# Fused attention and two gated MLPs on one core: the reciprocal root of two blocks' norms as a power on GpSimd

## The chip, the cores and the metric

The kernel runs on one core of one Trainium2 chip (trn2). A core has four engines that compute, each with a queue of its own that it works through in order: TensorE (PE in the rows; PEld is its loading of weights), VectorE (DVE), ScalarE (ACT) and GpSimd (POOL). SyncE (SP) issues the transfers (DMA). They wait for each other by semaphores. The metric is the device time of one launch in microseconds, the median of several runs.

## The reference

A windowed attention (4 batches, 8 heads, 576 positions of 64), a root-mean-square norm and a gated MLP with SiLU over its 2304 tokens of 512, and a second gated MLP without a norm. Cut to what matters:

```python
def _attn_ref(q, k, v):
    scores = (1.0 / np.sqrt(D)) * np.matmul(q, k.transpose(0, 1, 3, 2))
    rel = pos[:, None] - pos[None, :]
    scores = np.where((rel >= 0) & (rel < 64), scores, -1000000000.0)
    attn = np.exp(scores - np.max(scores, axis=-1, keepdims=True))
    attn = attn / (np.sum(attn, axis=-1, keepdims=True) + 1e-09)
    return np.matmul(attn, v)

def _moe_ref(x, w_gate, w_val, w_out, rms_g):
    rms = np.sqrt(np.mean(x * x, axis=-1, keepdims=True) + 1e-06)
    xn = x / rms * rms_g
    g = xn @ w_gate
    silu = g * (1.0 / (1.0 + np.exp(-g)))
    return silu * (xn @ w_val) @ w_out

def _moe2_ref(x, w_gate, w_val, w_out):
    gate = 1.0 / (1.0 + np.exp(-(x @ w_gate)))
    return gate * (x @ w_val) @ w_out
```

The weights are 512 x 1536 (gate and value) and 1536 x 512 (out). The change touches the factor 1 / rms of the norm.

## The kernel before

**Tiles and stages.** The 2304 tokens are six blocks of 384. Activations lie with the features on the 128 partitions (four groups of 128) and the tokens along the row. Attention makes 128 tokens at a time: scores on TensorE (L406), softmax on VectorE and ScalarE (L413 to L431), transposes (L439) and the product with v (L476), whose output ScalarE copies (L478) and squares (L481). Then comes the norm, then the first MLP, then the second. Blocks 0 and 1 take their first MLP by plain products, gate and value for one slice of 128 features of the 1536 at a time (L576, 12 products of 128x384 for either, since each number is split into a high and a low half of 16 bits); the later blocks, and the second MLP, take a scheme of fewer products over pairs of blocks (L625 to L627, L782, L893).

**Weights.** The weights arrive in chunks of 1024 columns and are readied on the way: VectorE takes the largest magnitude of each partition (L244), GpSimd reduces it over the partitions (an all-reduce, L247), VectorE turns that into a power of two (L248 to L255), and ScalarE and VectorE split the chunk into two halves (L271 to L273 and L337, L339). In block 0 and 1's time VectorE does this for one chunk after another.

**The norm of blocks 0 and 1** is `rms_first`, called for 256 tokens and for 128 tokens of each block, so four times: TensorE sums the squares into one column for each 128 tokens (L519), VectorE scales the sum and adds 1e-6 (L521, tile ra, 128x2 or 128x1), and `rsqrt` turns it into the reciprocal root (tile ry): an integer estimate and two corrections, ten VectorE operations on 128x2 or 128x1 numbers (L446 to L456, helpers rh and rt). VectorE multiplies the identity by it (L527), TensorE spreads that over the partitions (L528), VectorE scales the activations (L531), and `split_first` makes their two halves (L536 on ScalarE, L537 on VectorE), which L576 reads. Blocks 2 to 5 use `rms_scale`, whose root over 128x384 stays on VectorE in either kernel.

**Gate and value.** For a slice f the products fill one of two banks of PSUM. ScalarE takes the tanh (L588), VectorE frees the gate's bank (L589) and the value's (L599), and ScalarE and VectorE split the result (L609, L610). The next slice's gate needs the bank that L589 frees, its value the bank that L599 frees.

**Order.** The text of the program does not set the order. A table of numbers (ORDER, 5478 entries) does: `arrange` lists the operations as they were written, reads the table and ties every operation to the one ahead of it on its engine. The table was made by a planner outside the file. GpSimd's queue holds the all-reduces (L247, L279, L653), and three large ones for later norms (L509). The tile mhalf, 128x1 numbers of -0.5, is set at L1055 and read by nothing before.

Of the kernel before, what the change touches and what calls it, by code (L numbers as in the profile page):

```python
# [112 lines left out]
def fused_kernel(ctx, tc, q, k, v, w_gate, w_val, w_out, rms_g, w2_gate, w2_val, w2_out, const16, const32, out, plan, asked):  # L113
# [1101 lines left out]
    'FmuT*1^i5rOwj$U6ooSbFDb1z%KCj;>Oj@xCuOr|w6#x}g!<|kE^_!VDivlw`_f~MLTw4ViQck`W37c2#6=Lf$=ljUA&6}iNTbl@4@|RxE56HLXk^)kH'
    'skz$Drxtaex1GP(5y_flEjk&+h5nU}2#&>oSZ@d6QvjqVrr()ivuc^J+OFCbL12oT-~YvQnk?Q8lWj5G>U)!Re(6{_8q=>V?9Ta%fmGj%uI&qUHMoLwv'
    'Y}AMgeHxMyb%d6?Q0w&lI_aLTc=2hJRhF4G-<g;s3m~}T0l~KiWYPT+D*wf0<uj^l1=9B1s=ufc9J9&PxQAf%bWCff&db0Nxc9&VR2##foF(+m1ySt_2'
    'ucgv{vU;iNLEFkg2NH6PhKOQK~ZMihdv_aI+LXxiA8(8!{srcv0(zkC7cRhsetf;{k~QsUt6mBGo8!q?AI<p$|btPE_YAr0SqYM3YoA?z~**g9u6Uglp'
    'V^`5JAXA(_6EMT9C-H8B%DNd@u?psob)uoP^iMJi7-6&EOpPa&rH)<vG8R-M$Y+NMO_4r&VmDdnT`9Q9f@0vSlDP_?HTfdpE7^^5cROH{s<NEMVNa<Cw'
    'B?H@-=A6RHC%+z*oUptzsYCIjJnNq*TXClYfZ$~woa_e~t=@ZqU;sCW+(_u+F6p$hZpm^B394oQ~1><Sn3+I<Wx}#>lg3;MP@g4e7Z#%3_24uj1N{L(D'  # L1220
    'JF#`O9n?BDH}X$90mv|___fuvWzVwh%i^sUoySq<)iFu3UH^$)=Jw)($z$)t&xRzf;jM+AgRT!f46~11I6pCQjr}Y8y^;FcF70&tZPV>{N1a&lYR%zS_'
    'SLpN`IQm*89`MJU1v#1)lU@;3-`JHJ@?S|4qnIhRh#1qbJuRyJU$4A;uiVzS4k#p^;G-%XieI4;^E4p_335BKc1aE*ZRlYx26%ge?Gr;=aW*GSt$eT+s'
    'WImVdWQBZXH;@kovDUHo4!+qB-d^svpH1l`B=FACFI4^!uXU8|jGbv6qKl@~msH(4X_Gvm@Uwae%KAs3Q&XnDWu*G`xHMeVPgs4i=dO!~9;K9NS>W2Oh'
    'Ycng)=q3Wrv04*1(%9phV7)7QR~57k4Tm4&OI-b1hvmT80t3e=;e$+0B^!0xf46wIKq!}YB-E^~Q41fVLUNkYLxX&y3j0w35S4KEf8p-q?;9Q#L6VCz)'
# [142 lines left out]
```

## Time and profile before

| what | us |
|---|---|
| median of three runs | 873.52 (873.34 to 874.28) |
| span of the profiled execution | 872.6 |
| TensorE busy | 846.4 (97%) |
| VectorE busy | 736.5 (84%) |
| ScalarE busy | 555.1 (64%) |
| GpSimd busy | 31.3 (4%) |

The profile is one execution. Busy time is the time in which an engine ran an instruction. Starts and durations of small instructions overlap by some 0.08 us, since the next one starts while the last one drains, so what an instruction costs its engine is read from its start to the next one's start. A row of the chain is a piece of the work that ended last, followed back from the end. "POOLq" is what GpSimd's sequencer does on its own, without its cores computing.

### The profile page before, as it was taken

How to read it: one execution, taken by the hardware profiler on the slowest of the kernel's cores; microseconds unless marked ns; L12 is line 12 of the kernel's file. 1: busy time of each engine (PE TensorE's matmuls, PEld its weight loads, DVE VectorE, ACT ScalarE, POOL GpSimd, SP SyncE). 2: the span in 40 equal slices, each digit the busy share in tenths (PEclk: the TensorE clock that was granted, in tenths of full speed). 3: DMA queues.
4: the chain of work that ended last, by engine and by line, in shares of the span. 5: the costliest groups of instructions: out<-in, count | busy, mean ns of one | idle time of the engine just before them, and what ended most of it. 6: DMA issues, size and time to landing. Idle time of an engine off the chain costs nothing.

```text
span 872.6 us, 15623 instructions
## 1 busy us (share of the span) xinstructions
PE 846.4 (97%) x6084; PEld 523.7 (60%) x6084; DVE 736.5 (84%) x1427; ACT 555.1 (64%) x1214; POOL 31.3 (4%) x42
## 2 busy tenths in 40 slices
PE   4599999999999999999999999999999999999998
PEld 3466666666666666656666666666566666666664
DVE  5999999899887897688889999989889787546695
ACT  5888877767577866356466576767667457335640
POOL 0000010101000101100000000000000000000000
PEclk9989999999999999999999999999999999999999
DMA  9666531232112033301423656527241112023034
GB/s 342 240 210 239 192 127 45 66 104 80 66 38 66 27 133 137 125 37 37 133 85 118 223 190 233 208 73 238 85 147 45 62 41 91 2 72 138 28 109 145
DMA packets 33193, 104.19 MB, mean 119 GB/s; under 512 B 3808, under 2 KB 11360, under 8 KB 27872
## 3 DMA queue, kind: packets, MB, share of 16 engines
q1 hardware_dynamic: 33120, 103.20, 34.0%
...
HBM read 82.35 MB, written 20.84 MB: 118 GB/s over the span
## 4 chain that ended last, share of the span: by engine, by line
PE 88%; DVE 8%; DMA 2%; ACT 1%; issue 0%; POOL 0%; SPq 0%; DVEq 0%; ACTq 0%; POOLq 0%
PE bank L782 45%; PE bank L893 14%; PE bank L576 10%; PE bank L625 4%; PE bank L626 4%; PE bank L627 4%; PE bank L406 2%; PE bank L476 2%; PE bank L439 1%; DMA att<-f 1%; DVE wmax L244 1%; DMA att<-in_q_dram 1%; DMA wl<-in_moe_w_gate_dram 1%; DVE wl L339 1%; DVE wl L273 1%
## 5 line engine op out<-in xcount | busy, mean ns | idle before, releaser
L782 PEld LDWEIGHTS <-wl 128*128 128x128 f16 x2520 | 246.0, 98 | 164.9 <-issue 2.1
L782 PE MATMUL bank<-att,wl 128*128 128x384 f16 x2016 | 338.1, 326 | 0.6 <-DVE att L710 0.3
L795 ACT ACTIVATE bank<-bank 128x384 f32<-128x384 f32 x120 | 56.9, 478 | 75.4 <-PE bank L782 31.3
L893 PEld LDWEIGHTS <-wl 128*128 128x128 f16 x756 | 74.0, 98 | 48.9
L576 PE MATMUL bank<-xhl,wl 128*128 128x384 f16 x576 | 97.6, 326 | 0.4 <-DVE th L589 0.4
L782 PE MATMUL bank<-xhl,wl 128*128 128x384 f16 x504 | 86.2, 326 | 0.6 <-DVE xo L785 0.6
L576 PEld LDWEIGHTS <-wl 128*128 128x128 f16 x576 | 55.5, 98 | 36.9 <-issue 1.3
L625 PE MATMUL bank<-wl,wl 128*128 128x384 f16 x192 | 62.7, 326 | 0.0
L626 PE MATMUL bank<-wl,wl 128*128 128x384 f16 x192 | 62.6, 326 | 0.0
L627 PE MATMUL bank<-wl,wl 128*128 128x384 f16 x192 | 62.6, 326 | 0.0
L337 ACT ACTIVATE wl<-wl,isc 128x1024 f16<-128x1024 f32 (+1 forms) x48 | 54.2, 1142 | 9.6 <-DVE wl L317 6.3
L893 PE MATMUL bank<-xhl,wl 128*128 128x384 f16 x264 | 51.6, 326 | 0.0
L244 DVE TENSOR_REDUCE wmax<-wl 128x1 f32<-128x1024 f32 x36 | 43.6, 1213 | 4.8 <-DMA wl<-in_moe_w_out_dram 2.5
L893 PE MATMUL bank<-wl 128*128 128x384 f16 x222 | 45.9, 326 | 0.0
L271 ACT ACTIVATE wl<-wl 128x1024 f32<-128x1024 f32 x36 | 41.4, 1153 | 6.5 <-DMA wl<-in_moe_w_out_dram 3.5
L429 ACT ACTIVATE sm<-sm,su 128x128 f32<-128x128 f32 x120 | 38.0, 388 | 8.9 <-DVE su L424 8.7
L422 ACT ACTIVATE sm<-sm,nm 128x128 f32<-128x128 f32 x96 | 37.3, 391 | 9.2 <-DVE nm L416 9.2
L627 PEld LDWEIGHTS <-wl 128*128 128x128 f16 x288 | 28.2, 98 | 18.6
L625 PEld LDWEIGHTS <-wl 128*128 128x128 f16 x288 | 28.2, 98 | 18.6 <-issue 1.2
L339 DVE SCALAR_TENSOR_TENSOR wl<-wl,isc,wl 128x1024 f16<-128x1024 f32 (+1 forms) x32 | 38.1, 1196 | 1.1 <-ACT wl L337 0.9
L626 PEld LDWEIGHTS <-wl 128*128 128x128 f16 x288 | 28.2, 98 | 17.2
L273 DVE SCALAR_TENSOR_TENSOR wl<-wl,wl 128x1024 int32<-128x1024 int32 x28 | 34.3, 1225 | 0.3
...
## 6 DMA issues: line engine op xcount, KB each, us to landing
wl<-in_moe_w_out_dram SPq DMA_DIRECT2D x15, 1024.0 KB, 5.4
wl<-in_moe_w_val_dram SPq DMA_DIRECT2D x13, 1024.0 KB, 5.2
wl<-in_moe_w_gate_dram SPq DMA_DIRECT2D x13, 1024.0 KB, 5.7
...
vn<-in_v_dram SPq DMA_DIRECT2D x27, 256.0 KB, 3.4
...
```

Source lines behind the costliest of these rows:

```text
L244: V.tensor_reduce(out=r1[:, i:i + 1], in_=wraw(layer, j + i)[:, :, 1].bitcast(F32), axis=AX.X, op=ALU.max, apply_absolute_value=True)
L271: A.activation(out=y.bitcast(F32), in_=hi.bitcast(F32), func=AF.Prelu, scale=2.0 ** -112, alpha=-2.0 ** 32)
L273: V.scalar_tensor_tensor(out=y if (layer, j) in PACKED else hi, in0=y, scalar=3, in1=lo, op0=ALU.logical_shift_left, op1=ALU.bitwise_or)
L337: A.activation(out=hi, in_=y, func=AF.Copy, scale=sc)
L339: V.scalar_tensor_tensor(out=lo, in0=y, scalar=sc, in1=hi, op0=ALU.mult, op1=ALU.subtract)
L576: T.matmul(pb[:, 0:n], lhsT=w_, rhs=x_, start=(c == 0), stop=(c == m - 1))
L625: T.matmul(o[c][:, 0:n], lhsT=wh[:, cs], rhs=hi, start=st, stop=False)
L626: T.matmul(o[c][:, 0:n], lhsT=wh[:, cs], rhs=lo, start=False, stop=False)
L627: T.matmul(o[c][:, 0:n], lhsT=wl[:, cs], rhs=hi, start=False, stop=en)
L782: T.matmul(pb[:, 0:NMAX], lhsT=w_, rhs=x[:, t, kk], start=first and kk == n == 0, stop=kk == 1 and n == 2, skip_group_check=not first)
L795: A.activation(out=o[:, 0:NMAX], in_=i[:, 0:NMAX], func=AF.Copy)
L893: T.matmul(pb[:, 0:NMAX], lhsT=w_, rhs=x[:, t], start=st and s == ss[0] and n == 0, stop=s == ss[-1] and n == 2, skip_group_check=not st)
```

## The change

In `rms_first` the call of `rsqrt` becomes one GpSimd instruction, a power: ra to the exponent -0.5, which is mhalf spread over the columns. It is L522 in either file, and is called four times. The ten operations L446 to L456 go from these four calls, and helpers rh and rt with them. The whole table ORDER is another one (its lines say nothing to a reader and are left out; of 5478 entries it places 4535 differently, by 12 places in the median).

```diff
--- before.py
+++ after.py
@@ -519,7 +519,7 @@
                 T.matmul(pb[:, i:i + 1], lhsT=sq_tile(blk, t0 + i)[:, c], rhs=ones[:, 0:1], start=(c == 0), stop=(c == KC - 1))
         a, y = small("ra", 3)[:, 0:nt], small("ry", 3)[:, 0:nt]
         V.tensor_scalar(out=a, in0=pb[:, 0:nt], scalar1=1.0 / DM, scalar2=1e-6, op0=ALU.mult, op1=ALU.add)
-        rsqrt(y, a, small("rh", 3)[:, 0:nt], small("rt", 3)[:, 0:nt], V)
+        G.tensor_tensor(out=y, in0=a, in1=mhalf.to_broadcast([P, nt]), op=ALU.pow)
 
         pb = abank(st, "r")
         for i in range(nt):
```

Since the buffers are numbered as they are made, names such as wmax_389 and wmax_367 are the same tile in both.

**GpSimd's queue from its first all-reduce.** Before, up to the third all-reduce (amax are the largest magnitudes of two weight chunks, gamr that of the norm's gain):

```order
L1302 MEMSET const-uint8-127 128x1
L1361 UNCONDITIONAL_BRANCH
L247 ISA
L247 ISA amax_83<-wmax_0_389 128x2
L279 ISA gamr_0_119<-gam_0_117 128x1
L247 ISA amax_83<-wmax_1_492 128x2
```

Now, from the third all-reduce to the seventh:

```order
L247 ISA amax_83<-wmax_1_470 128x2
L522 ISA
L522 TENSOR_TENSOR ry_1_356<-ra_1_355,mhalf_82 128x1
L522 TENSOR_TENSOR ry_0_305<-ra_0_304,mhalf_82 128x2
L247 ISA
L247 ISA amax_83<-wmax_0_367 128x2
...
L522 ISA
L522 TENSOR_TENSOR ry_0_305<-ra_0_304,mhalf_82 128x2
L247 ISA
L247 ISA amax_83<-wmax_1_470 128x2
```

An ISA row with no tile stands wherever a power follows an all-reduce or an all-reduce a power; there are six such rows besides the first one, and the kernel before has that first one alone. The power of block 1's first two tiles (ra_0_304) stands ahead of an all-reduce of two chunks that has no wait of its own, since it follows in the queue.

**VectorE's queue at block 0's norm.** Before, from the L521 of its first 256 tokens (ra_304, ry_305; ra_366, ry_367 are those of the third 128):

```order
L521 TENSOR_SCALAR ra_304<-bank_200 128x2
L272 TENSOR_SCALAR wl_76<-wl_76 128x1024
L446 TENSOR_SCALAR ry_305<-ra_304 128x2
L339 SCALAR_TENSOR_TENSOR wl_75<-wl_76,isc,wl_75 128x1024
L447 TENSOR_SCALAR ry_305<-ry_305 128x2
L521 TENSOR_SCALAR ra_366<-bank_126 128x1
L449 TENSOR_TENSOR rh_307<-ry_305 128x2
L446 TENSOR_SCALAR ry_367<-ra_366 128x1
```

Now, from the L521 of the third 128 tokens (now ra_355, ry_356):

```order
L521 TENSOR_SCALAR ra_355<-bank_126 128x1
L339 SCALAR_TENSOR_TENSOR wl_75<-wl_76,isc,wl_75 128x1024
L418 TENSOR_SCALAR nm_183<-nm_183 128x8
L527 TENSOR_SCALAR xhl_266<-ident,ry_356 128x128
L521 TENSOR_SCALAR ra_304<-bank_200 128x2
L339 SCALAR_TENSOR_TENSOR wl_75<-wl_76,isc,wl_75 128x1024
L527 TENSOR_SCALAR xhl_266<-ident,ry_305 128x128
```

The third tile comes first, and one L339 stands between each L521 and the L527 that needs its power.

**VectorE's queue at block 1's first norm call.** Before, from its L521 (th are gate and value results, wl2 weights and halves):

```order
L521 TENSOR_SCALAR ra_0_304<-bank_0_125 128x2
L589 SCALAR_TENSOR_TENSOR th_0_474<-th_0_474,bank_4_200 128x384
...
L446 TENSOR_SCALAR ry_0_305<-ra_0_304 128x2
L610 TENSOR_TENSOR wl2_76<-th_1_540,wl2_76 128x384
L447 TENSOR_SCALAR ry_0_305<-ry_0_305 128x2
...
L244 TENSOR_REDUCE wmax_0_389<-wl2_76 128x1
...
L273 SCALAR_TENSOR_TENSOR wl2_76<-wl1_75,wl2_76 128x1024
```

Now:

```order
L521 TENSOR_SCALAR ra_0_304<-bank_0_125 128x2
L244 TENSOR_REDUCE wmax_0_367<-wl2_76 128x1
L610 TENSOR_TENSOR wl2_76<-th_0_452,wl2_76 128x384
L272 TENSOR_SCALAR wl2_76<-wl2_76 128x1024
L248 TENSOR_SCALAR amax_83<-amax_83 128x2
L255 TENSOR_SCALAR tg1_86<-pw_84,pgam_81 128x1
L599 SCALAR_TENSOR_TENSOR th_1_518<-th_1_518,bank_5_206 128x384
```

The L248 now stands three rows behind the L244 that follows L521, and on GpSimd its all-reduce stands behind this call's power. L599 of the same slice follows it.

**VectorE's queue at block 1's second norm call.** Before, from the L244 of the chunk, with the L521 and the L527 of the call:

```order
L244 TENSOR_REDUCE wmax_1_492<-wl2_76 128x1
L339 SCALAR_TENSOR_TENSOR wl1_75<-wl2_76,isc_85,wl1_75 128x1024
...
L521 TENSOR_SCALAR ra_1_366<-bank_2_163 128x1
...
L599 SCALAR_TENSOR_TENSOR th_2_616<-th_2_616,bank_5_206 128x384
...
L456 SCALAR_TENSOR_TENSOR ry_1_367<-rh_1_369,ry_1_367 128x1
L527 TENSOR_SCALAR xhl_3_526<-ident_77,ry_0_305 128x128 x2
L589 SCALAR_TENSOR_TENSOR th_1_540<-th_1_540,bank_4_200 128x384
L527 TENSOR_SCALAR xhl_3_526<-ident_77,ry_1_367 128x128
```

Now, from the L244 to the L527:

```order
L244 TENSOR_REDUCE wmax_1_470<-wl2_76 128x1
L339 SCALAR_TENSOR_TENSOR wl1_75<-wl2_76,isc_85,wl1_75 128x1024
L589 SCALAR_TENSOR_TENSOR th_0_452<-th_0_452,bank_4_200 128x384
L610 TENSOR_TENSOR wl2_76<-th_1_518,wl2_76 128x384
L527 TENSOR_SCALAR xhl_3_504<-ident_77,ry_0_305 128x128
L248 TENSOR_SCALAR amax_83<-amax_83 128x1
L521 TENSOR_SCALAR ra_1_355<-bank_2_163 128x1
L599 SCALAR_TENSOR_TENSOR th_0_452<-th_0_452,bank_5_206 128x384
L423 TENSOR_SCALAR su_0_146<-su_0_146 128x8
L527 TENSOR_SCALAR xhl_3_504<-ident_77,ry_1_356 128x128
```

The L244's all-reduce, the power of ra_1_355 and the L527 that reads it (ry_1_356) are nine rows apart on VectorE, and the power stands on GpSimd behind that all-reduce and one ISA row.

## Rows read from the trace of the kernel before

**Rows 1.** The page's busy shares (1) and its chain by engine (4).

```profile
PE 846.4 (97%) x6084; PEld 523.7 (60%) x6084; DVE 736.5 (84%) x1427; ACT 555.1 (64%) x1214; POOL 31.3 (4%) x42
...
PE 88%; DVE 8%; DMA 2%; ACT 1%; issue 0%; POOL 0%; SPq 0%; DVEq 0%; ACTq 0%; POOLq 0%
```

**Rows 2.** Table by stretches: busy us of each engine, granted clock, DMA share, GB/s.

```profile
core 0: us, PE busy (x) PEld busy (x) DVE busy (x) ACT busy (x) POOL busy (x), PEclk, DMA share, GB/s
...
20.00:30.00 10.00, 5.42 (x48) 4.32 (x47) 10.00 (x25) 8.96 (x24) 0.73 (x1) 1.00 0.81 296
...
40.00:51.20 11.20, 7.54 (x80) 5.55 (x79) 11.12 (x36) 9.24 (x23) 0.72 (x1) 0.56 0.62 221
...
75.00:100.00 25.00, 25.00 (x216) 16.82 (x214) 24.87 (x58) 20.52 (x47) 1.09 (x3) 1.00 0.40 141
100.00:125.00 25.00, 25.00 (x210) 16.01 (x208) 24.68 (x59) 18.80 (x48) 2.15 (x3) 1.00 0.61 224
...
850.00:872.60 22.60, 19.07 (x118) 11.25 (x115) 13.00 (x24) 2.21 (x5) 0.00 (x0) 1.00 0.41 140
```

**Rows 3.** Chain of waits in the head: start us, us, what.

```profile
43.28 0.28 DVE xhl L527
...
51.30 8.72 PE bank L576 x53
```

**Rows 4.** The page's costliest groups (5): out<-in, count, busy us, mean ns, idle before.

```profile
L337 ACT ACTIVATE wl<-wl,isc 128x1024 f16<-128x1024 f32 (+1 forms) x48 | 54.2, 1142 | 9.6 <-DVE wl L317 6.3
...
L271 ACT ACTIVATE wl<-wl 128x1024 f32<-128x1024 f32 x36 | 41.4, 1153 | 6.5 <-DMA wl<-in_moe_w_out_dram 3.5
...
L339 DVE SCALAR_TENSOR_TENSOR wl<-wl,isc,wl 128x1024 f16<-128x1024 f32 (+1 forms) x32 | 38.1, 1196 | 1.1 <-ACT wl L337 0.9
```

**Rows 5.** VectorE's timeline, three places: start us, us, line, operation, out<-in.

```profile
85.28 0.55 DVE L610 TENSOR_TENSOR wl<-th,wl 128x384 f16<-128x384 f32 x1
85.75 0.15 DVE L449 TENSOR_TENSOR rh<-ry 128x2 f32<-128x2 f32 x1
85.82 1.22 DVE L244 TENSOR_REDUCE wmax<-wl 128x1 f32<-128x1024 f32 x1
86.95 0.16 DVE L450 TENSOR_TENSOR rh<-rh,ra 128x2 f32<-128x2 f32 x1
...
99.09 0.69 DVE L272 TENSOR_SCALAR wl<-wl 128x1024 int32<-128x1024 int32 x1
99.70 0.15 DVE L451 TENSOR_SCALAR rt<-rh 128x1 f32<-128x1 f32 x1
...
118.43 0.55 DVE L589 SCALAR_TENSOR_TENSOR th<-th,bank 128x384 f32<-128x384 f32 x1
```

**Rows 6.** TensorE's timeline, gate and value products from 111 us.

```profile
111.40 17.72 PE L576 MATMUL bank<-xhl,wl 128*128 128x384 f16 x108
```

**Rows 7.** The line of the all-reduces, L247: min/median/max ns, starts, who waited.

```profile
L247 POOL PARTITION_ALL_REDUCE amax<-wmax x30: 350/584/1311, 16.5 to 705.7; - x30
L247 POOLq MODIFY_POOL_CONFIG  x2: 11/11/11, 0.8 to 0.8; - x2
...
  DVE amax L248: 1.7, 5
```

**Rows 8.** GpSimd's timeline: start us, us, line, operation.

```profile
0.27 0.10 POOL L1302 MEMSET const-float32-1.0<- 128x1 f32 x1
...
16.48 0.81 POOL L247 PARTITION_ALL_REDUCE amax<-wmax  x1 [16.06 <-DVE su L423]
...
87.13 0.37 POOL L247 PARTITION_ALL_REDUCE amax<-wmax  x1 [10.29 <-DVE rh L450]
```

**Rows 9.** DMA issues of the first 60 us: KB each, median us to landing.

```profile
wl<-in_moe_w_gate_dram SPq DMA_DIRECT2D x5, 1024.0 KB, 5.7
...
att<-in_q_dram SPq DMA_DIRECT2D x6, 256.0 KB, 5.6
...
wl<-const SPq DMA_DIRECT2D x1, 128.0 KB, 2.0
```

More of the change, by code (lines that the diff above doesn't have):

```diff
@@ L1215 @@
[L1215 to L1224, printed above, removed]
@@ L1255 @@
[L1255 to L1259 removed]
+    'c-n1O2S5}@7rvR@+v6G>2X_Z3N0TBQLhl9?0Z~j8H5ywq8oMSY8jYzYL4Qj$CeheyEV0DirHBP3(g{)oL5lQ#Wq1As<Zk!y;P$r6o0;#u?|tvBSF>3&kjfBL'
@@ new lines @@
+    'LrbXPNuX1y1ANh7)c`+5Fdsrp%EcToE6ky`i88mYX^zH>F{%6>9Q8D8^c`uw7yn5Yj7p$xPC2vaFg5~{U?!LgCV^1cE9=2*A_0Yl!}BoV-fO$pSi+qcjTl$='
+    'h&3Z_QqJAbT~%xK?vqVRjI%@V8h)_@^eqm_Z49|(Vubr$_M;a!qM|Y>YiJ@e!W+z0V#Umq4x`<R+s%-o0$0AW>E)9`s+TVYo$_93lVIZY(GN{Zkx<lOYz*2>'
+    'JOIfB;vP}o4=$Di2%vF~Rzh(j;Qb(&7YNBKSln<F1E}3_-u|WN&v}np=t0q`eHP=did)RKrP$Sa#GD52p96S&I-&>^r%4qDJn?}lAw5|K-eE~`DV_&a+u$oC'
+    'yLtZ4v_PS}KmA0=GkPLiL}5_cg8N{vdTlWXC;@_B>;yO|>V6IVin{}2_bLR%4uuj0x7e@SI7h+d@o<Vqw#s0;qKS+1yKo>t2vb%oP1{X7wWcK3p&YmCN40aF'
@@ new lines @@
+    '07ISyz_V~9)d#X=7=|hVoSso-Q;qCG5!G{U)*I}$mE}&#+aL-{rJ@1O2h~b&YSs2+U`=L@ut-g62c{jjC!F)m8CRV<;h1pZ3xuIh_AI~<elg+KPxwivF~CJg'
+    'gTHqJK};Qc50AXx%|*v&f^OsBEWDYoIX)A|H4yShT#ex*4gr7=sf8*WLT7a;?znh2ns#dX@gFx#5x1I9YN4&D0Jkt}k#zb#6>>qRPlacj8U3Iuv>?1KUD7ED'
+    'ZIpIMTcsczTv5*g*Fr$jJv8w!NV*F;6UoeRfe*UHW6nrGrzE;X(kyF+Lf`yWJib#S<-RTmfA@maBTeci$!d;oHN~2w!B?k&6XVeJ(OI!JRqc|t&_}LRwSAQv'
+    'qPi&QaO3B#A|(_-Z95_F?T|vX{DnF4s-TJDo*`>>t+J7%Ms%vVLbb@g%!#V>?39quH`Tqs1Srk&T0eYd)}k^qLd~9yn7L<8Gpw~T8<y_{UbNvMg)Uf=9JQh7'
@@ new lines @@
+    'G>Os_Hba1k;qaQ4uukzq*T}ovm##JiVrW|+QktSd3oZ~iDjJ{_nMtFXohof}Y_C&DDg!FTidPD5Jy5Dz8@ohZB1z5g_XK-^QH?p6yU820fBl_t&@Gf0q<WnF'
+    'PWH;Q?1j4*KHa+3XUZAXb5Ld}EU)`?n?-|S!>RvV(i9CgRmrF2Yd_tU&v)vrEOJwFwbv#{9e2b(tFxSRHR-d66&32-<TKNAdG`My@1ji}iyJG0E?D|rDf;rf'
+    'C+|*plrZCQ&?6JeNU5s1KIvd|?-P47t`-n2V|FhDH)1;~)GzBlJmnSo$CG`HW%3*TPr89XZj%Q1F~;Wu+xA!dx^+|Xfw|P-#));r!*O+9MUUcpA14>u2`a5*'
+    'b<ZO*t^S_gDrk)Xe@z2t-v_PPe#5+TRB5ZT6cE8YTdrdxcu=~e)Rj)6CK2GKdP#w#+yT^C{=TsZn3cDS&0trT0%QgJ71!Dw-~vcc0s!y?xea1LFaOKQ5%rL7'
@@ new lines @@
+    '90&hNgm!V^0Hdbyj?A?EZ)EXtezH~X<liDd`acvlVM+9RVYFGom9;;EHBoW&>6P)+b0^9M2!LZ-`~N<-zC6hjV1(GVtlgwThN*{DFGSbk_mNI`@DV$HP)0a-'
+    'MmXco-KKv-+cr}ju3+ZRxJQA<hv>7dN6Y{ieJh^I56C9D`(Ceq2}UYse7}BEvxQ2_GaUx=++lKC0e<N-lT5z&f}>^K(`n$+M8Z1DN)0Z8DQz;ptoGPqM=qXD'
+    'XiPvrrwK-^4M#CjdZk*UwD4gkr_K#YNINu}zQzE#5`Peo6+uxMnGta$Fv3)T+cz@h8}NRS0GuSQKgkBV4~9_0{V)g!Eew4u>h>(-+XY-9!T2Lq^G`I16*s|H'
+    'lAq_6?ih&OI}N^lgrp8dQ4PYh1r_TLT}Zmu7}93iC?~yA7HR#m`RQ`klEl^FE_cV>AgQt8->=QE8(!{~0Yd~&18&G(3e7#H&xa-<$D<Y}xXE6%p1t$fxBlY%'
@@ new lines @@
+    'ihtD?e>}mT=zJVU^T>9SVh^Iu`{TObzuN^yj?8FEn32Bs#F1Z!NAUV9P*`Uv%bak>$VSldN^Sj5tXpPiq5RWrX!&|Y=R+h*{&LO{a`J<*Xn(&ao+L_$+9T#o'
+    'A0CA>4-w&)79EN$8TG4+>&@XGoTh3%mF^+!sWG=71&!G^`^OC>=~$ra<?&a+gK3jiSvZA*jTRL<*Z!P5J8#^Lglo!4o7QR}zRc=W4i>jj4SlT}&}{xWlfPz='
+    'yaO95Q4v`8o_qGS33JCk*zCJA^*_qeK1&f;R6ZkyIQ>$2Aqk$?l689g2mku23o3epN=KcMN4~;U+~@5f@}}6!50h*UtOQuoi$L3Q-i4(lHxiGf6k?C7&7=G`'
+    'Rc$N^{$lg(AL1gzw7D&#ww5`D_^*~lE|?y>V)Oi&5yUm(^DHfK=Rzu><)uX5io#A~)b?2?KG-Ytd?aW!RT-&PWrENxYi{OWY&E+Ws`&eU(TZ(uKi*1%8!3LS'
@@ L1260 @@
+    'tY&~+J6S$py|5S*T1Ipzpj&0&lv!a05A6o8ME&)R@fwBoiB|uo6R`<m&{J{xE47|}j5iLJ5*juz%;tfks}TeL1KdDpU@%*l3~Pa51I7UcjrM?A4AcpvD;kC`'
+    'LjMO`Dvy%'
 )
```

63 lines of the change are left out of this document (24 added, 39 removed).

## The prediction

> **What bounds the kernel now.** I read the page's busy shares and its chain first. TensorE is busy for 846.4 of 872.6 us and carries 88% of the chain that ended last, VectorE 8% [rows 1]. The table by stretches then says where TensorE's missing 26 us lie [rows 2]: in the head, up to its first gate product L576 at 51.30 us [rows 3], and in the last 22.6 us, where 3.5 us are missing. Between them TensorE is full. It is full there only because VectorE keeps up: VectorE is busy 11.12 of 11.2 us before the first L576, 24.87 of 25 us from 75 to 100 and 24.68 of 25 from 100 to 125 [rows 2]. The margin is read from two timelines. The 108 products from 111.40 us take 17.72 us, so the 12 of one bank 1.97, and the fifth dozen starts at 111.40 + 4 x 1.97 = 119.28 [rows 6]; the L589 that frees its bank ends at 118.43 + 0.55 = 118.98 [rows 5]. So TensorE is 0.3 us from waiting for VectorE. Up to about 127 us a microsecond of VectorE is a microsecond of the program; after that TensorE is full to the end, and what was lost or won stays.
>
> The profiled span is 872.6 us, the median of the runs 873.52. All sums below are differences, added to the median.
>
> **Part 1: forty VectorE instructions go.** Four calls of ten. One of them holds VectorE from 85.75 to 85.82, so 0.07 us from start to start, and now and then somewhat more for a turn of tiles [rows 5]: 40 x 0.075 = 3.0 us, half in the head, half between 82 and 102 us. At the tight places near 119 to 127 us the new order also keeps one L272 (0.61 us, from 99.09 to 99.70 [rows 5]) behind instead of ahead. VectorE thus has 3.0 to 3.6 us less to do before it frees those banks.
>
> **Part 2: the new order in the head.** Up to block 0's last L537 VectorE now has, besides the 20 instructions gone (1.5 us), two L244 (85.82 to 86.95, 1.13 us each), two L272, one L273 and one L339 (1.2 us [rows 4], the L273 alike) less in front: 1.5 + 2.3 + 1.2 + 1.2 + 1.2 and 0.2 of small ones = 7.6 us. ScalarE, which makes the squares that L519 sums and was busy 8.96 of 10 us in the stretch from 20 us [rows 2], sheds two L337 and one L271 there, 1.14 + 1.14 + 1.15 = 3.4 us [rows 4]. So VectorE will wait for ScalarE and TensorE in the head: not at all if ScalarE sets nothing, 7.6 - 3.4 = 4.2 us if it sets everything. Its products serve one of several steps there, so I take a third, 1.4 us. The first L576 should come 4 to 6 us earlier, near 46 us. This gain is mostly not kept: the work pushed behind the norm is still VectorE's, TensorE starts early and then meets the same evictions, which are only 3.0 to 3.6 us less late. Kept: 3.5 - 1.4 = **-2.1 us**. The order's shuffling after 130 us moves no work between engines; TensorE is full there, and I put it at nothing, within 2 us either way. The tail is the same chain of products, eviction and store.
>
> **Part 3: what the power costs on GpSimd.** The power itself is 128 x 1 or 128 x 2 numbers. No row shows it. The nearest are GpSimd's MEMSET of 128 x 1, 0.10 us [rows 8], and its all-reduces of 128 x 1 or 2, 0.35 to 1.31 us [rows 7]; I take 0.6 with the two hand-overs. That replaces a chain of ten instructions, and in the head an L339 (1.2 us) stands between each L521 and its L527, so it costs nothing there.
>
> The larger cost is not in the diff. In the changed order GpSimd has six more of the ISA rows that carry no tile, one wherever a power follows an all-reduce or the reverse; the kernel before has one, ahead of its first all-reduce. There the trace calls it MODIFY_POOL_CONFIG, 11 ns on GpSimd's sequencer at 0.8 us [rows 7]: GpSimd is switched to another set of routines. What such a switch costs until the next routine can run, call it X, lies between 0.011 us and the 15.65 us that pass from there to the first all-reduce at 16.48 us, which waited for its data, not for the switch [rows 7, 8]. If routines have to be fetched, the nearest rows are loads: 2.0 us for a small constant tile, 5.6 and 5.7 us for tiles of the first 60 us [rows 9]. I take X = 5.6, as most loads there take that, and as routines for a whole engine are not a small tile.
>
> The Trainium skill, GPSIMD Engine Reference, section 2.1 (Instruction dispatch), says that the first call to freshly loaded code pays some 6 us (5.95 measured) for loading, with no instruction to be seen. No row here shows it; with 5.95 in place of X the forecast below would be 880.1 us.
>
> Which switches are covered? In the head the switch before the first power has some 8 us between the all-reduce ahead of it and the L521 that it waits for, and the one after the second power some 7 us until the next L248 asks for an all-reduce: hidden at 5.6. In block 1 two are not.
> (a) L521 of the first two tiles, then a power, a switch, and the all-reduce of weight chunk 10, on which an L248 waits three VectorE instructions later: L244 1.13, L610 0.47, L272 0.61 [rows 5], 2.21 us of cover. Needed: 0.6 + X + 0.37 (an all-reduce like that at 87.13 [rows 8]). Exposed: X - 1.24.
> (b) The all-reduce of chunk 13 behind its L244, a switch, the power of the third tile, and its L527. In VectorE's queue between that L244 and that L527 stand an L339 (1.2 [rows 4]), three of 0.47 (L589, L610, L599) and four small ones, 3.0 us in all. Needed: 0.37 + X + 0.6. Exposed: X - 2.0.
> Behind both waiting instructions, in the same queue, stand L589 and L599, which free the banks of TensorE's gate and value products; nothing else covers them. Today all L248 together wait 1.7 us [rows 7]. Together 2X - 3.2, which is 8.0 us at 5.6. TensorE has more slack than 0.3 us at about 90 us, but by 119 to 127 us it has used it, so the wait arrives there whole.
>
> **Sum.** 873.5 - 2.1 + 8.0 = **879.4 us**. Every 1 us of X is 2 us; the sum is no change at X = 2.7.
>
> **Rivals.**
> *A, faster: the switch is short or fetched ahead.* If X is below 1.2 us both waits vanish in their cover and the 40 instructions are simply gone: 873.5 - 2.1 = 871.4, 870 to 872 by the head's term. For it: the one row there is reads 11 ns, and no queue of loads on the page is named for it. It decides from X below 1.7.
> *B, slower by more: the routines are fetched only when first called, not at the switch.* Then the cover ahead of a call is lost. In the head the first power of block 0 pays X + 0.6 less the L339 and L418 between its L521 and L527, 1.3: X - 0.7. In block 1 place (a) pays twice, 2X - 1.2, and at (b) only 0.6 us stand between L521 and L527: X. Together 4X - 1.9 = 20.5 us at 5.6, less 2.1: about 892, or 888 where TensorE's slack at 90 us takes some. For it speaks nothing in the trace: the first all-reduce took 0.81 us [rows 8], no longer than others, but it came long after the switch. The rule of that page of the skill, read by its letter (the first call pays), is this case.
> *C, no change: X near 2.7*, like the small constant's load [rows 9]: 871.8 to 875.3.
> *D, the gain is not there:* if the path in the head is ScalarE's and TensorE's wholly, 4.2 us are waited for instead of 1.4 and the kept gain is nothing: every case is 2 us later, A is C.
>
> **How the numbers follow.** Forecast, X from 3.5 to 8: 0.48. A 0.26, C and A with D 0.12, B 0.14. A measurement of this kernel can tell about 0.2%, 1.75 us, from no change, so faster (under 871.8) 0.26, same 0.12, slower 0.62. The forecast's own range is 875.5 to 885. For 8 in 10 the range has to take in most of A, so it starts at 870.5; B is left out above, and it ends at 885.5.
>
> **What would show it.** First L576 near 46 us (part 2). GpSimd idle between an all-reduce and the power, though the L521 has ended, by X; VectorE idle near 85 to 90 us ahead of an L248 by about 4.4 us, and near 103 to 107 us ahead of an L527 by about 3.6. TensorE idle before L576 between 90 and 127 us by some 6 us, and full after. If VectorE stands idle ahead of the first L527 of block 0, it is B. If VectorE waits nowhere for GpSimd, it is A. What would make all of it wrong: a fall of the granted clock after the new pauses (it stood at 0.56 over the sparse 40 to 51 us [rows 2]), or stages after 130 us whose new order makes TensorE wait.

## The result, and the profile after

The changed kernel takes 885.94 us (median of 4 runs, 884.86 to 886.3) where the kernel before takes 873.9 beside it: 1.0135 of its time, with an interval of 1.0121 to 1.0149, so 12.0 us slower. The direction was forecast and so was the mechanism; the size was not: 879.4 us was predicted, and the range ended at 885.5.

The page of the changed kernel, its busy shares and the group of the gate and value products:

```profile
PE 850.4 (96%) x6084; PEld 524.4 (59%) x6084; DVE 729.1 (82%) x1387; ACT 550.0 (62%) x1214; POOL 32.3 (4%) x46
...
L576 PE MATMUL bank<-xhl,wl 128*128 128x384 f16 x576 | 102.5, 336 | 4.0 <-DVE th L599 3.0
```

The span grew by 11.5 us, from 872.6 to 884.1. TensorE has the same 6084 products. It stands still for 884.1 - 850.4 = 33.7 us where it stood still for 26.2 [rows 1], so 7.5 us more, and it is busy 4.0 us longer with the same work.

The table by stretches of the changed kernel, with the columns of [rows 2]:

```profile
40.00:51.20 11.20, 11.20 (x108) 7.48 (x101) 10.81 (x19) 9.42 (x19) 0.62 (x1) 0.78 0.45 166
51.20:75.00 23.80, 22.62 (x192) 14.12 (x190) 23.80 (x42) 20.61 (x45) 0.71 (x2) 1.00 0.58 214
75.00:100.00 25.00, 21.83 (x184) 14.33 (x183) 19.80 (x36) 18.43 (x51) 1.79 (x3) 0.93 0.47 162
100.00:125.00 25.00, 16.35 (x138) 10.30 (x137) 14.08 (x33) 9.47 (x25) 1.61 (x3) 0.80 0.38 127
```

Three things stand in it. VectorE, which was busy 24.87 and 24.68 of 25 us from 75 to 125 us [rows 2], is now busy 19.80 and 14.08. TensorE, full before, loses 3.2 and 8.6 us there, and already 1.2 us from 51.2 to 75. And its granted clock falls to 0.93 and 0.80 in those stretches, where it was 1.00.

What VectorE waited for is in its timeline (the bracket says how long it stood idle, and what ended that), at the two places of block 1:

```profile
85.88 0.69 DVE L272 TENSOR_SCALAR wl<-wl 128x1024 int32<-128x1024 int32 x1
91.31 0.17 DVE L248 TENSOR_SCALAR amax<-amax 128x2 f32<-128x2 f32 x1 [4.74 <-POOL amax L247]
...
91.51 0.55 DVE L599 SCALAR_TENSOR_TENSOR th<-th,bank 128x384 f32<-128x384 f32 x1
...
101.59 0.55 DVE L599 SCALAR_TENSOR_TENSOR th<-th,bank 128x384 f32<-128x384 f32 x1
102.05 0.17 DVE L423 TENSOR_SCALAR su<-su 128x8 f32<-128x8 f32 x1
111.02 0.29 DVE L527 TENSOR_SCALAR xhl<-ident,ry 128x128 f32<-128x128 f32 x1 [8.80 <-POOL ry L522]
```

The first is the L248 of chunk 10, 4.74 us; the second the L527 of the third tile, 8.80 us. Both end with GpSimd. GpSimd's own timeline of the same stretch shows why:

```profile
62.84 0.36 POOL L247 PARTITION_ALL_REDUCE amax<-wmax  x1 [5.56 <-DVE wmax L244]
84.01 0.74 POOL L522 TENSOR_TENSOR ry<-ra,mhalf 128x2 f32<-128x2 f32 x1 [20.81 <-DVE ra L521]
90.90 0.37 POOL L247 PARTITION_ALL_REDUCE amax<-wmax  x1 [6.16 <-issue]
99.32 1.32 POOL L247 PARTITION_ALL_REDUCE amax<-wmax  x1 [8.05 <-DVE wmax L244]
110.40 0.59 POOL L522 TENSOR_TENSOR ry<-ra,mhalf 128x1 f32<-128x1 f32 x1 [9.76 <-issue]
116.94 0.38 POOL L247 PARTITION_ALL_REDUCE amax<-wmax  x1 [5.96 <-issue]
```

After the power that ends at 84.01 + 0.74 = 84.75 the all-reduce of chunk 10, whose data were there before 84 us, starts at 90.90: a switch back takes 6.15 us. After the all-reduce that ends at 99.32 + 1.32 = 100.64 the power starts at 110.40, though its L521 was done by 101.7: a switch to the power takes 9.76. The next one back takes 116.94 - 110.99 = 5.95. The switch itself stands on GpSimd's sequencer, two records for each, with 1 to 85 ns where [rows 7] has 11, and nothing else is recorded of it:

```profile
L522 POOLq MODIFY_POOL_CONFIG  x6: 83/85/85, 23.6 to 100.6; - x6
```

```profile
L247 POOLq MODIFY_POOL_CONFIG  x6: 1/5/11, 36.1 to 111.2; - x6
```

In the head TensorE's first L576 comes at 43.44 us, 7.9 us earlier than in [rows 3]:

```profile
43.44 4.82 PE L576 MATMUL bank<-xhl,wl 128*128 128x384 f16 x24
```

and behind the two pauses:

```profile
92.11 5.74 PE L576 MATMUL bank<-xhl,wl 128*128 128x384 f16 x24 [3.00 <-DVE th L599]
...
112.81 4.01 PE L576 MATMUL bank<-xhl,wl 128*128 128x384 f16 x12
...
117.53 2.11 PE L576 MATMUL bank<-xhl,wl 128*128 128x384 f16 x12
```

The last three of these lines are the second cost of the waits. A dozen products took 2.11 us at 117.53, but 4.01 at 112.81, straight behind the long pause; and the two dozen at 92.11, behind the pause at the first place, took 5.74 instead of some 4, at a granted clock of 0.73 from 94 to 98 us. The granted clock (the third number from the right) of the stretch behind the long pause was 0.54, close to the lower of its two levels (1.2 GHz, against 2.4):

```profile
113.00:117.00 4.00, 4.00 (x17) 2.09 (x15) 2.94 (x9) 1.92 (x7) 0.06 (x1) 0.54 0.77 258
117.00:123.00 6.00, 6.00 (x75) 3.99 (x77) 4.94 (x8) 4.89 (x7) 0.32 (x1) 1.00 0.16 50
```

Together the two dozen and the one dozen take some 3.7 us more than at full clock (1.8 and 1.9). The whole group of gate and value products takes 102.5 us (the page's row above); in the kernel before it took 4.9 less (the head's first two dozen, 4.82 us at 43.44, are 0.9 of this):

```profile
L576 PE MATMUL bank<-xhl,wl 128*128 128x384 f16 x576 | 97.6, 326 | 0.4 <-DVE th L589 0.4
```

### The profile page after: what moved, and what is told of

It reads as the page before. It is cut to its first block, busy times and chain, and to the rows that moved or that the text cites. A ratio compares the mean times of both kernels' runs of the same rounds, so it can differ in the third digit from the quotient of the medians.

```text
span 884.1 us, 15608 instructions
## 1 busy us (share of the span) xinstructions
PE 850.4 (96%) x6084; PEld 524.4 (59%) x6084; DVE 729.1 (82%) x1387; ACT 550.0 (62%) x1214; POOL 32.3 (4%) x46
## 3 DMA queue, kind: packets, MB, share of 16 engines
q1 hardware_dynamic: 33120, 103.20, 33.7%
## 4 chain that ended last, share of the span: by engine, by line
PE 76%; DVE 13%; ACT 4%; DMA 4%; issue 3%; POOL 1%; SPq 0%; ACTq 0%; POOLq 0%; DVEq 0%
PE bank L782 41%; PE bank L893 14%; PE bank L576 5%; PE bank L625 4%; PE bank L627 4%; PE bank L626 4%; DMA f<-xhl 2%; DVE wl L339 2%; DVE wl L273 1%; PE bank L406 1%; PE bank L439 1%; PE bank L476 1%; DVE wmax L244 1%; DVE th L589 1%; DMA att<-f 1%
## 5 line engine op out<-in xcount | busy, mean ns | idle before, releaser
L576 PE MATMUL bank<-xhl,wl 128*128 128x384 f16 x576 | 102.5, 336 | 4.0 <-DVE th L599 3.0
L782 PE MATMUL bank<-xhl,wl 128*128 128x384 f16 x504 | 86.1, 326 | 0.1
L576 PEld LDWEIGHTS <-wl 128*128 128x128 f16 x576 | 57.0, 101 | 43.7 <-issue 9.8
L893 PE MATMUL bank<-xhl,wl 128*128 128x384 f16 x264 | 52.1, 326 | 0.0
L244 DVE TENSOR_REDUCE wmax<-wl 128x1 f32<-128x1024 f32 x36 | 43.5, 1211 | 3.7 <-DMA wl<-in_moe_w_out_dram 3.7
L339 DVE SCALAR_TENSOR_TENSOR wl<-wl,isc,wl 128x1024 f16<-128x1024 f32 (+1 forms) x32 | 38.0, 1196 | 3.0 <-ACT wl L337 2.8
L273 DVE SCALAR_TENSOR_TENSOR wl<-wl,wl 128x1024 int32<-128x1024 int32 x28 | 34.2, 1220 | 0.5 <-ACT wl L271 0.5
```

Source lines behind the costliest of these rows:

```text
L244: V.tensor_reduce(out=r1[:, i:i + 1], in_=wraw(layer, j + i)[:, :, 1].bitcast(F32), axis=AX.X, op=ALU.max, apply_absolute_value=True)
L273: V.scalar_tensor_tensor(out=y if (layer, j) in PACKED else hi, in0=y, scalar=3, in1=lo, op0=ALU.logical_shift_left, op1=ALU.bitwise_or)
L339: V.scalar_tensor_tensor(out=lo, in0=y, scalar=sc, in1=hi, op0=ALU.mult, op1=ALU.subtract)
L576: T.matmul(pb[:, 0:n], lhsT=w_, rhs=x_, start=(c == 0), stop=(c == m - 1))
L782: T.matmul(pb[:, 0:NMAX], lhsT=w_, rhs=x[:, t, kk], start=first and kk == n == 0, stop=kk == 1 and n == 2, skip_group_check=not first)
L893: T.matmul(pb[:, 0:NMAX], lhsT=w_, rhs=x[:, t], start=st and s == ss[0] and n == 0, stop=s == ss[-1] and n == 2, skip_group_check=not st)
```

## The experiments

All changes of order below are changes of the table alone, shown as rows of an engine's queue. A ratio is the time over that of the kernel before, run beside it.

**Is it the two waits, or the order? (e_both)** GpSimd's queue is regrouped so that block 1 has one switch to the power and one back:

```diff
 L247 ISA amax_83<-wmax_0_367 128x2
+L247 ISA amax_83<-wmax_1_470 128x2
 L522 ISA
 L522 TENSOR_TENSOR ry_0_305<-ra_0_304,mhalf_82 128x2
-L247 ISA
-L247 ISA amax_83<-wmax_1_470 128x2
-L247 ISA amax_83<-wmax_1_470 128x1
-L522 ISA
 L522 TENSOR_TENSOR ry_1_356<-ra_1_355,mhalf_82 128x1
 L247 ISA
+L247 ISA amax_83<-wmax_1_470 128x1
```

The readers on VectorE move with it.

> The changed kernel with its instructions and its table as they are, but for these places of the table: on GpSimd the all-reduce of chunk 10 stands ahead of block 1's first power and that of chunk 13 behind block 1's second power, so that block 1 has one switch to the power and one back, not two of each; on VectorE the readers are moved to fit (the first L527 of block 1 beside its second, the L521 of the third tile three rows earlier, L248 and L249 of chunk 13 some 25 rows later). Theory (the waits of VectorE for GpSimd's switches, 4.74 us ahead of the L248 at 91.3 and 8.80 us ahead of the L527 at 111.0, are the whole loss): both waits go, 885.9 - 13.5 = 872.4 us, and faster than before by 0.5 to 2 us. Rival (the new order loses time by itself, in the head where the granted clock was 0.71 to 0.78, or after 130 us): above 876 us, with TensorE idle elsewhere.

Measured: 870.57 us, ratio 0.9955 (0.9939 to 0.9972). Run again (e_both5):

> The table of e_both once more, for a closer interval. Theory (start of TensorE earlier by the new order, and 40 VectorE operations less: both are needed, and both are there): 0.995 to 0.997 of the kernel before, 870 to 872 us. Rival (the first measure was chance): 0.998 to 1.000.

871.16 us, ratio 0.9961 (0.9948 to 0.9973). So the same four powers, with the same new order of the head, are faster than the kernel before by 3.4 to 3.9 us, and faster than the changed kernel by some 15. The waits, with what followed from them, were the loss. GpSimd in e_both over the same stretch:

```profile
85.32 0.35 POOL L247 PARTITION_ALL_REDUCE amax<-wmax  x1 [20.21 <-DVE wmax L244]
93.15 0.73 POOL L522 TENSOR_TENSOR ry<-ra,mhalf 128x2 f32<-128x2 f32 x1 [7.47 <-DVE sm L415]
97.99 0.81 POOL L522 TENSOR_TENSOR ry<-ra,mhalf 128x1 f32<-128x1 f32 x1 [4.11 <-DVE ra L521]
108.93 0.89 POOL L247 PARTITION_ALL_REDUCE amax<-wmax  x2 [10.13 <-issue]
```

The power of the third tile now follows the first one without a switch; it waits for its L521, not for its routines. The first power does wait for them (its L521 ended at 85.76), and so does the all-reduce at 108.93, but nothing on VectorE reads either result that early: the switches lie where nobody asks. The lengths are worth a look: 85.67 to 93.15 there, at most 7.5, and 98.80 to 108.93 back, 10.1, where the changed kernel's took 6.

**Each wait alone (e_a, e_b).** In e_a only chunk 10's all-reduce moves ahead of block 1's first power; six switches stay.

```diff
 L247 ISA amax_83<-wmax_0_367 128x2
+L247 ISA amax_83<-wmax_1_470 128x2
 L522 ISA
 L522 TENSOR_TENSOR ry_0_305<-ra_0_304,mhalf_82 128x2
 L247 ISA
-L247 ISA amax_83<-wmax_1_470 128x2
 L247 ISA amax_83<-wmax_1_470 128x1
```

> The changed kernel with only the first of the two moves: the all-reduce of chunk 10 ahead of block 1's first power, and the first L527 of block 1 beside its second. All six switches stay. If the two waits are separate prices that add up, 4.74 us go: 881.2 us. If GpSimd's queue of switches sets the end (83.4 us, then 9.8 to the power, 0.7, 6.1 back, 0.4, 9.8 again, so the last power near 110 us as now), the wait only moves to the L248 of chunk 13 and the L527 behind it: 885 to 886 us.

881.24 us, ratio 1.0078 (1.006 to 1.0095): the value of the theory in which the two prices add up. The trace says that this is only half its merit. The first wait is gone, but VectorE waits 1.62 us at the next L248, as the chain of switches foretold, and the second wait is 7.62 us in place of 8.80. That is 4.3 us of waiting less in all, and the two dozen products that took 5.74 us in the changed kernel took 4.07 here (from 88.83 us):

```profile
86.08 0.16 DVE L248 TENSOR_SCALAR amax<-amax 128x2 f32<-128x2 f32 x1
...
98.07 0.15 DVE L248 TENSOR_SCALAR amax<-amax 128x1 f32<-128x1 f32 x1 [1.62 <-POOL amax L247]
...
106.45 0.29 DVE L527 TENSOR_SCALAR xhl<-ident,ry 128x128 f32<-128x128 f32 x1 [7.62 <-POOL ry L522]
```

The chain of switches was the right picture, only with shorter links than I gave it: 7.51 and 7.79 us to the power in place of 9.8 twice.

In e_b only chunk 13's all-reduce moves, behind block 1's second power:

```diff
 L247 ISA amax_83<-wmax_1_470 128x2
-L247 ISA amax_83<-wmax_1_470 128x1
 L522 ISA
 L522 TENSOR_TENSOR ry_1_356<-ra_1_355,mhalf_82 128x1
 L247 ISA
+L247 ISA amax_83<-wmax_1_470 128x1
```

> The changed kernel with only the second of the two moves: the all-reduce of chunk 13 behind block 1's second power, with L521 of that call and L248 and L249 of chunk 13 moved on VectorE. The first wait (4.74 us at the L248 of chunk 10) stays; the switch ahead of the second power then begins at 91.3 and is over at 101.1 us, when L521 is just done. Both theories of the switches: 885.9 - 8.8 = 877 us. Rival (the order itself loses): above 880.

875.48 us, ratio 1.0014 (1.0002 to 1.0026), 10.6 us less than the changed kernel, where 8.8 were expected. With the long pause the lower clock behind it is gone too, which was worth 1.9 us (4.01 against 2.11 for a dozen); the columns are those of [rows 2]:

```profile
100.00:125.00 25.00, 24.68 (x205) 15.53 (x204) 24.67 (x53) 16.94 (x44) 2.70 (x6) 1.00 0.62 222
```

**The order without the power (v_dve10).** The changed kernel's table, with the ten VectorE operations put back in all four calls:

```diff
-        G.tensor_tensor(out=y, in0=a, in1=mhalf.to_broadcast([P, nt]), op=ALU.pow)
+        rsqrt(y, a, small("rh", 3)[:, 0:nt], small("rt", 3)[:, 0:nt], V)
```

> The changed kernel's table with the ten VectorE operations put back for all four calls, spread over the rows between L521 and the first L527 of each call; no power and no switch but the first. Theory (the switches are the whole loss): VectorE has its 3.0 us again, and the time is that of the kernel before or up to 2 us over it, 873.5 to 875.5 us. Rival (the order loses time by itself): above 878 us.

875.11 us, ratio 1.0005 (0.9996 to 1.0015): the new order alone neither wins nor loses. Its table by stretches:

```profile
51.20:75.00 23.80, 22.51 (x191) 14.10 (x190) 23.80 (x42) 20.56 (x44) 0.71 (x2) 1.00 0.61 224
75.00:100.00 25.00, 23.99 (x207) 15.80 (x205) 24.81 (x56) 21.34 (x59) 2.02 (x3) 1.00 0.58 198
100.00:125.00 25.00, 23.59 (x197) 14.59 (x196) 24.55 (x57) 16.45 (x41) 1.29 (x3) 1.00 0.58 212
```

TensorE starts its first L576 at 45.64 us, 5.7 earlier than before, and gives 3.7 of it back by 125 us (1.29, 1.01 and 1.41 in these rows): it waits while VectorE is as good as full. The other 2 us are not in these stretches; TensorE was busy for 848.3 us in this execution, where it was busy 846.4 before.

**The power without the order (v_b1).** The kernel before with its own table; only block 1's calls are powers, both in the gap of GpSimd's queue from 92 to 118 us:

```diff
-        rsqrt(y, a, small("rh", 3)[:, 0:nt], small("rt", 3)[:, 0:nt], V)
+        if blk == 0:
+            rsqrt(y, a, small("rh", 3)[:, 0:nt], small("rt", 3)[:, 0:nt], V)
+        else:
+            G.tensor_tensor(out=y, in0=a, in1=mhalf.to_broadcast([P, nt]), op=ALU.pow)
```

> The kernel before with its own table, where only block 1's two calls (20 VectorE operations) become powers, both of them on GpSimd between the all-reduces of chunks 13 and 15, so in a gap from 92.0 to 117.9 us that holds one switch there and one back; the setting of -0.5 is moved to VectorE's sixth place. Theory (a covered switch costs nothing, and the operations are worth what they hold VectorE for): 1.4 us less, or 0.9984 of the kernel before, less what the first L527, at 102 us, may still wait for the switch (0 to 1.5 us). Rival (the gain of e_both is the new order's, not the power's): no change or slower by up to 0.2%.

874.55 us, ratio 1.0002 (0.9993 to 1.001). My theory fell here: the switch was covered (the powers run at 96.95 us), and VectorE is less full, but nothing came of it:

```profile
75.00:100.00 25.00, 25.00 (x216) 16.76 (x215) 24.22 (x47) 20.60 (x47) 2.83 (x5) 1.00 0.45 164
100.00:125.00 25.00, 25.00 (x210) 15.97 (x208) 24.13 (x53) 19.16 (x47) 2.31 (x4) 1.00 0.55 202
```

TensorE is full in these stretches, as it was before [rows 2]. VectorE's work is worth something only once TensorE could run ahead of it, and for that TensorE has to start earlier. Together with v_dve10: the earlier start without the lighter VectorE is worth nothing, the lighter VectorE without the earlier start is worth nothing, both together 3.4 to 3.9 us. Two things limit this reading: v_b1 lightens VectorE by block 1's twenty operations alone, and e_both has the regrouped all-reduces besides, which v_dve10 has not.

**Half of it (v_half).** The changed kernel's table, block 0 with the power, block 1 with the ten operations:

```diff
-        G.tensor_tensor(out=y, in0=a, in1=mhalf.to_broadcast([P, nt]), op=ALU.pow)
+        if blk == 0:
+            G.tensor_tensor(out=y, in0=a, in1=mhalf.to_broadcast([P, nt]), op=ALU.pow)
+        else:
+            rsqrt(y, a, small("rh", 3)[:, 0:nt], small("rt", 3)[:, 0:nt], V)
```

> The changed kernel's table with block 0's two calls as powers and block 1's two calls as ten VectorE operations each, spread between L521 and L527; one switch to the power and one back, both in the head. Theory (with the new order TensorE starts earlier, and from then on VectorE's work sets the pace, so every operation taken off it counts, in the head as in block 1): half of what e_both wins over v_dve10, 2 us less than the kernel before, 0.9978. Rival (only operations in block 1 count, since in the head VectorE waits for ScalarE anyway): 0.9995 to 1.0005.

872.92 us, ratio 0.9983 (0.9973 to 0.9992): 1.5 us, some half of the whole, as the theory had it. With the new order, operations count in the head as well as in block 1.

**What a switch costs (v_probe).** The kernel before with two chains of dummy instructions that nobody waits for (p is a power, r an all-reduce, m a multiply; ten in a stretch with dense transfers, six behind GpSimd's last work):

```diff
+        for i, o in enumerate("pprrppmrmr" "prprpr"):
+            d = dum[:, i:i + 1]
+            if o == "r":
+                G.partition_all_reduce(d, pgam, channels=P, reduce_op=RED.max)
+            else:
+                G.tensor_tensor(out=d, in0=pgam, in1=mhalf, op=ALU.pow if o == "p" else ALU.mult)
```

> The kernel before, with two chains of dummy instructions of 128x1 on GpSimd whose results nothing reads: after the all-reduce at 515.6 us, where transfers are dense, power, power, all-reduce, all-reduce, power, power, multiply, all-reduce, multiply, all-reduce; and behind GpSimd's last instruction, where they are sparse, power, all-reduce, power, all-reduce, power, all-reduce. Nothing waits for them. Theory (a switch is a load of routines, started at the switch): each first instruction after a switch comes 5.5 to 10 us late, a second one of the same kind at once; the multiply needs the power's switch too; where transfers are dense a switch takes longer than where they are sparse. Rival (the length goes by direction alone: 9.8 us to the power, 6 us back): the same two lengths in both chains. The time stays that of the kernel before within 0.3%.

874.33 us, ratio 0.9996 (0.9983 to 1.0009). GpSimd's timeline, both chains (L1209 is power and multiply, L1207 the all-reduce; x2 and x3 are runs without a switch):

```profile
514.01 0.35 POOL L248 PARTITION_ALL_REDUCE amax<-wmax  x1 [1.24 <-DVE wmax L245]
522.77 1.75 POOL L1209 TENSOR_TENSOR dum<-pgam,mhalf 128x1 f32<-128x1 f32 x2 [8.41 <-issue]
530.38 0.85 POOL L1207 PARTITION_ALL_REDUCE dum<-pgam  x2 [5.86 <-issue]
538.33 1.78 POOL L1209 TENSOR_TENSOR dum<-pgam,mhalf 128x1 f32<-128x1 f32 x3 [7.09 <-issue]
546.51 0.83 POOL L1207 PARTITION_ALL_REDUCE dum<-pgam  x1 [6.40 <-issue]
558.00 1.23 POOL L1209 TENSOR_TENSOR dum<-pgam,mhalf 128x1 f32<-128x1 f32 x1 [10.67 <-issue]
566.23 0.38 POOL L1207 PARTITION_ALL_REDUCE dum<-pgam  x1 [6.99 <-issue]
```

```profile
712.08 0.81 POOL L1209 TENSOR_TENSOR dum<-pgam,mhalf 128x1 f32<-128x1 f32 x1 [7.02 <-issue]
718.65 0.38 POOL L1207 PARTITION_ALL_REDUCE dum<-pgam  x1 [5.76 <-issue]
726.59 0.99 POOL L1209 TENSOR_TENSOR dum<-pgam,mhalf 128x1 f32<-128x1 f32 x1 [7.56 <-issue]
733.41 0.38 POOL L1207 PARTITION_ALL_REDUCE dum<-pgam  x1 [5.83 <-issue]
740.95 0.59 POOL L1209 TENSOR_TENSOR dum<-pgam,mhalf 128x1 f32<-128x1 f32 x1 [7.17 <-issue]
747.84 0.75 POOL L1207 PARTITION_ALL_REDUCE dum<-pgam  x1 [6.30 <-issue]
```

With few transfers the switch to the power took 7.02, 7.56 and 7.17 us, the one back 5.76, 5.83 and 6.30. With many it was 8.41, 7.09 and 10.67, and 5.86, 6.40 and 6.99. So both theories are right in part: the direction makes about 1.3 us where transfers are few, and four of the six switches among many transfers are longer than those. The contrast of the two chains is not sharp: the DMA share was 0.47 to 0.67 during the first six switches and 0 to 0.58 during the last six. A second instruction of the same kind comes at once. A plain multiply needs the power's switch: the 10.67 us is ahead of one.

**What makes a switch longer (v_load).** The 10.67 us switch in the probe began at 547.34, 0.2 us behind the issue of a 1 MB load (547.16); the 9.76 us switch of the changed kernel at 100.64, 0.2 us behind one too (100.44). The load was moved; it is then issued at 110.30 us, behind the switch, and the load of v that followed it stands ahead of it, near 90 us:

```diff
-L234 DMA wl2_76<-in_moe_w_out_dram 128x2048
-L372 DMA vn_1_348<-in_v_dram 128x512
-L234 DMA wl2_76<-in_moe_w_out_dram 128x2048
+L372 DMA vn_1_348<-in_v_dram 128x512
+L234 DMA wl2_76<-in_moe_w_out_dram 128x2048 x2
```

> The changed kernel with one transfer moved on SyncE: the 1 MB load that it issued at 100.44 us, 0.2 us ahead of the switch to block 1's second power, is issued behind the next 1 MB load, at 112.7 us. Theory (a switch that is issued just behind a 1 MB load waits for it): the switch takes 7 to 7.8 us in place of 9.76, the power comes 2 to 2.7 us earlier, and the time is 883.2 to 884 us, 1.0105 to 1.0115 of the kernel before. Rival (its length is chance or goes by the place): 9.8 us and 1.0135.

883.29 us, ratio 1.0098 (1.0083 to 1.0112). The switch ends at 107.92 after 7.56 us:

```profile
99.03 1.32 POOL L247 PARTITION_ALL_REDUCE amax<-wmax  x1 [8.05 <-DVE wmax L244]
107.92 0.59 POOL L522 TENSOR_TENSOR ry<-ra,mhalf 128x1 f32<-128x1 f32 x1 [7.56 <-issue]
```

The power comes 2.2 us sooner, and the time is lower than the changed kernel's by 0.37%, 3.2 us, which is 2.2 within the two intervals. Part of the 3.2 may be the clock: in this execution it did not fall behind the first pause, though that was as long as in the changed kernel (2.86 us against 3.00), and a dozen products took 2.11 us:

```profile
91.82 2.11 PE L576 MATMUL bank<-xhl,wl 128*128 128x384 f16 x12 [2.86 <-DVE th L599]
```

So without transfers issued beside it this switch was 2.2 us shorter. The move took away two of them, the 1 MB load at 100.44 and the 256 KB load of v at 100.82, and which of the two held it up is not shown. Nor is nearness to a 1 MB load the whole rule. The long switches back in e_both fit it (98.80 us is 1.4 us behind such a load at 97.40), but in the probe the switch back that began at 559.23, 1.1 us behind a 1 MB load at 558.12, took only 6.99. What decides the length among transfers stays open.

**VectorE beside GpSimd (v_head).** In the head the two powers took 1.57 and 1.68 us, in block 1 0.59 and 0.74. Beside each of the long ones VectorE ran an L339 (from 31.97 and from 34.02 us). In v_head these are moved behind the L527:

```diff
 L521 TENSOR_SCALAR ra_0_304<-bank_4_200 128x2
-L339 SCALAR_TENSOR_TENSOR wl1_75<-wl2_76,isc_85,wl1_75 128x1024
 L527 TENSOR_SCALAR xhl_1_266<-ident_77,ry_0_305 128x128
+L339 SCALAR_TENSOR_TENSOR wl1_75<-wl2_76,isc_85,wl1_75 128x1024
```

> The table of e_both, with the two L339 that stand between L521 and L527 of block 0 each moved behind that L527, so that VectorE is idle while the two powers of block 0 run. Theory (a GpSimd instruction is held up while VectorE runs an L339): the two powers take 0.6 to 0.75 us each as in block 1, not 1.57 and 1.68, and VectorE waits some 0.7 us for each, as much as it saves; the time is that of e_both within 0.3%. Rival (the powers of block 0 are long since they are the first after their load): still 1.6 us, and the head 1 to 2 us later.

871.37 us, ratio 0.9966 (0.9955 to 0.9976), that of e_both within its interval. The powers take 0.60 and 0.70 us:

```profile
31.83 0.60 POOL L522 TENSOR_TENSOR ry<-ra,mhalf 128x1 f32<-128x1 f32 x1 [8.44 <-DVE ra L521]
34.09 0.70 POOL L522 TENSOR_TENSOR ry<-ra,mhalf 128x2 f32<-128x2 f32 x1 [1.66 <-DVE ra L521]
```

A GpSimd instruction beside an L339 does not end before it. (The all-reduce at 99.32 in the changed kernel, 1.32 us in place of 0.37, ran beside an L339 too.) Not every VectorE instruction does this: the power at 85.27 us in e_b took 0.74 beside an L244, whose one input is a tile of the same size. Nor does it take a 16-bit result: an all-reduce of the changed kernel at 694.77 us took 1.38 beside an L273, whose result has 32 bits.

## Why the prediction was wrong in its size

*What bounds the kernel* held: TensorE is full only because VectorE keeps up, and a wait put into VectorE's queue near 90 to 105 us reaches TensorE and stays. But the sentence that up to 127 us a microsecond of VectorE is a microsecond of the program holds in one direction only. More work on VectorE delays a TensorE with 0.3 us of slack; less work there did not speed one that is already full (v_b1).

*Parts 1 and 2, the gain*: forecast 2.1 us, measured 3.4 to 3.9 (e_both, e_both5; that the changed kernel keeps as much is taken from there). The first L576 came at 43.44, not near 46: 7.9 us earlier, as much as the 7.6 us of work that part 2 takes from VectorE ahead of it. The term that was mis-sized is the 1.4 us that VectorE should wait for ScalarE and TensorE in the head. The list of VectorE's waits in e_both from 20 to 51.2 us has two lines, and neither is for ScalarE:

```profile
DVE xhl L527 <- POOL ry L522: 1.0, 2, 0.6
DVE ra L521 <- PE bank L519: 0.3, 1, 0.3
```

The first is for the powers, made long by L339. That a part of the gain at the first L576 is lost again came as described, but not to VectorE's evictions alone: of the 1.2 us of TensorE from 51.2 to 75 us, 0.59 is ahead of the products at 53.94, for the bank that L589 frees, and 0.59 ahead of an L476 at 68.78, for ScalarE's L441.

*Part 3* is the step that failed, in one number. The reading that the six rows without a tile are switches, that they cost time of which their row of 11 ns says nothing, that two of them are uncovered and which two, and that the other four are hidden, all held. X did not: I gave all switches one X of 5.6 us. Measured:

| place | forecast | measured wait | what it is made of |
|---|---|---|---|
| (a) L248 of chunk 10 | X - 1.24 = 4.4 | 4.74 | switch back 6.15 |
| (b) L527 of the third tile | X - 2.0 = 3.6 | 8.80 | switch to the power 9.76, all-reduce 1.32 for 0.37 |
| both | 8.0 | 13.5 | |

By the prediction's own formulas, with 6.15 and 9.76 in place of X, the waits are 4.9 and 7.8, together 12.7; the 0.95 us by which the all-reduce of chunk 13 was longer beside an L339 makes up the rest. The sum would then have been 873.5 - 2.1 + 12.7 = 884.1. The row was chosen too low for the switch to the power, and one X for both directions was wrong: to the power it took 6.68 us in v_b1, 7.0 to 7.6 in the probe's sparse chain and 7.56 in v_load.

*The clock* was named only as what would make all wrong. It is a term of this sum: TensorE lost some 3.7 us behind the two pauses, where the granted clock was near its lower level (0.54 behind the long one). The account is: 13.5 us of waits, less 3.4 to 3.9 of kept gain, gives 9.6 to 10.1; 12.0 were measured; the 2 us that are left are no more than those 3.7, of which the gaps that TensorE had anyway took a part. That split is worked out, not measured by itself, and it rests on one profiled execution; in v_load's the clock did not fall behind the first pause.

*The rivals.* A, a switch that is short or fetched ahead, fell. B, routines fetched only at the first call, fell on block 1's first power: its switch began when the all-reduce at 62.84 had ended, and 20.8 us later the power took 0.74 us, as short as any, straight behind its L521; v_probe's second instructions show the same from the other side. C, an X near 2.7, falls with A, and D, no gain from the new order and the lighter VectorE, falls on e_both. The Trainium skill, GPSIMD Engine Reference, section 2.1 (Instruction dispatch), puts the loading of fresh code at 5.95 us and lays it on the first call. The switches back agree with the size (5.76 to 6.30 us in the probe's sparse chain, 5.95 and 6.15 in the changed kernel), those to the power are longer, and the wait begins at the switch, not at the first call. That a small GpSimd instruction lasts longer beside some VectorE instructions was no term at all; it shows as waits of 0.4 and 0.6 us in the head and as 0.95 us of the second wait. In the head it decided nothing: v_head, with short powers, takes the time of e_both.
